# Tokens for the later experts turned by VectorE after a trip through DRAM, in place of TensorE transposes

## Chip, cores and metric

The kernel runs on one core of a Trainium2 chip. The metric is the time of one execution on the device in microseconds, the median over the runs shown.

## What is computed

Chunked attention is followed by a layer of eight experts, of which each token uses one. All is float32.

```python
# attention, chunk by chunk of 32 queries (4 batches, 8 heads, 768 positions, 64 wide)
k_full = concatenate([mem_k, k[l_start:r_end]]); v_full likewise
a = softmax(scale * q_c @ k_full.T)
out[chunk] = a @ v_full
# experts: x is the attention's output as 3072 tokens x 512
logits = x @ w_gate + modality_bias[modality_id]
e_idx = argmax(logits, 1)
gate_w = softmax(logits)[e_idx]
for e in range(8):
    h = maximum(x[e_idx == e] @ w1[e], 0)          # 512 -> 1024
    out[e_idx == e] = gate_w * (h @ w2[e])         # 1024 -> 512
```

## The kernel before

The attention runs first and leaves the tokens, with their gates, as rows of 516 floats in a DRAM scratch `xd`. Then the expert stage works in *slots*. A slot takes 256 tokens of one expert. A plan that the kernel computes on the chip, the table of *rows*, says for each row which expert and which 256 tokens it stands for, and whether its weights differ from those already loaded. Rows have fixed numbers: 0 to `HEAD` = 3, then up to eight rows of half-full tails (none here), `ROW_R1` = 12, `ROW_X` = 13, up to seven extra rows behind it (14 to 17 are used here), and 33 and 34. While a slot computes one row, it prepares the next one. So the slot that the code calls `slot(13)` prepares row 13; the last call, `slot(None)`, prepares nothing. Two slots also carry a *rest* of up to 32 more tokens; `spread` is a small constant matrix that lays these out over 128 partitions.

In a slot, `mm1(f)` for f = 0 to 7 multiplies the tokens with one eighth of `w1`: 12 matmuls, as each float32 operand is split into a rounded part and a remainder (`wh` and `wl` for weights, `xth` and `xtl` for tokens, `hh` and `hl` for what comes out) and three of the four products are taken. `mm2(f)` multiplies with `w2`, six matmuls for each f. `conv(i)` makes `wh` and `wl` of one of 16 tiles of weights `raw`: ScalarE copies, VectorE subtracts.

The tokens of the next row come by two indirect DMAs (`gather`, GpSimd's queue) into `xg`, with one token on each partition. The contraction needs them the other way round, the 512 channels on partitions. So `trans(half)` has TensorE transpose four 128x128 blocks into PSUM, from where ScalarE makes `xth` and VectorE `xtl`. This is done in `prepare(f)`, behind `mm2(2)` and `mm2(3)`.

Each engine runs its instructions in the order in which the code writes them. At a slot's head stands `begin(row)`: SP issues the loads of the next row's `w1` (`load_w(row, 0)`), ScalarE writes the finished tokens times gate to `outs` (`finish`), GpSimd scatters them to the output (`store`), copies indices and gates of the row now due (`keep`), and gathers the next row. SP's loads of `w2` (`load_w(row, 1)`) come behind `mm1`. A load waits until the conversion of what is in its buffer is through.

Of the kernel before, what the change touches and what calls it, by code (L numbers as in the profile page):

```python
# [9 lines left out]
F32 = mybir.dt.float32  # L10
F32R = mybir.dt.float32r
BF16 = mybir.dt.bfloat16
I32 = mybir.dt.int32
U32 = mybir.dt.uint32
AF = mybir.ActivationFunctionType
# [5 lines left out]
P = 128  # L21
# [25 lines left out]
NR = 32  # L47
# [5 lines left out]
def tile_chunk_attention_top1_moe(  # L53
# [31 lines left out]

    xd = dram.tile([N, XW], F32, name="xd")
    qf = q.rearrange("b h s d -> (b h s) d")
    kf = k.rearrange("b h s d -> (b h s) d")
# [100 lines left out]
    regs0 = const.tile([1, 2], I32, name="regs0")  # L189
    tab_i = const.tile([P, 193], I32, name="tab_i")  # L190
    ohg = const.tile([P, E], F32, name="ohg")

# [6 lines left out]
    def more_constants():  # L199
# [53 lines left out]
        for at in (63.5, 95.5):  # L253
            nc.vector.tensor_scalar(edge, pcol, at, None, op0=ALU.is_gt)
            nc.vector.tensor_add(quarter, quarter, edge)
            yield "v"
        nc.vector.tensor_copy(mod_f, mod_i[:, :, 0])
        yield "v"
    def bias_rows():
# [431 lines left out]
    raw, wh, wl = [None] * 16, [None] * 16, [None] * 16  # L691
    w1h, w1l = [xa.tile([P, 8, 512], F32R, name=f"w1{i}") for i in range(2)]
    for f in range(8):
        raw[f] = xa.tile([P, 512], F32, name=f"raw{f}")
        wh[f], wl[f] = w1h[:, f], w1l[:, f]
    xp = hp = xg = xth = xtl = ix = gx = hh = hl = None
    ix_now = const.tile([P, 2], I32, name="ix_now")
    gate_now = const.tile([P, 2], F32, name="gate_now")
    ev = {}

    def load_w(row, half):
        if half == 0:
            if row == 0:
                ev[0] = nc.values_load(regs0[0:1, 0:1], engines=[mybir.EngineType.SP], min_val=0, max_val=E - 1,
                                       skip_runtime_bounds_check_because="the place of one of 8 experts")
            else:
                r = (regs1 if row < 2 else regs)[row:row + 1]
                ev[row] = nc.values_load(r[:, 0:1], engines=[mybir.EngineType.SP], min_val=0, max_val=E - 1,
                                         skip_runtime_bounds_check_because="the place of one of 8 experts, or 0")
                ev[row, "c"] = nc.values_load(r[:, 1:2], engines=[mybir.EngineType.SP], min_val=0, max_val=1,  # L710
                                              skip_runtime_bounds_check_because="a comparison gives 0 or 1")
        e = ev[row]
        kw = {} if row == 0 else {"cond": ev[row, "c"]}
        for f in range(8):
            if half == 0:
                nc.sync.dma_start(
                    raw[f].rearrange("p (c f) -> p c f", f=P),
                    w1[ds(e, 1), :, f * P:(f + 1) * P].rearrange("o (c p) f -> p (o c) f", p=P), **kw)
            else:
                nc.sync.dma_start(raw[8 + f], w2[ds(e, 1), f * P:(f + 1) * P, :].rearrange("o p d -> p (o d)"), **kw)  # L720
# [5 lines left out]

    def keep():
        nc.gpsimd.tensor_copy(ix_now, ix)  # L728
        for t in range(2):
            nc.gpsimd.tensor_copy(gate_now[:, t:t + 1], xg[t][:, DM:DM + 1])  # L730
# [13 lines left out]
    def gather_rest(i):  # L744
# [7 lines left out]
        nc.gpsimd.tensor_copy(own_r[i], ixr[i])  # L752

    def trans(half):
        t = bank().rearrange("p (c n) -> p c n", c=2)
        for cc in range(2):
            for tt in range(2):
                c = 2 * half + cc
                nc.tensor.transpose(t[:, cc, tt * P:(tt + 1) * P], xg[tt][:, c * P:(c + 1) * P], ident)  # L759
        sl = slice(2 * half, 2 * half + 2)  # L760
        nc.scalar.copy(xth[:, sl, 0:256], t)  # L761
        nc.vector.tensor_sub(xtl[:, sl, 0:256], t, xth[:, sl, 0:256].bitcast(F32))

# [6 lines left out]

    def mm1(f, rest=False):
        w = 256 + (NR if rest else 0)
        pw = bank()[:, 0:w]
        ph = pw[:, 0:256]

        for n in range(12):
            wt, x, c = ((wh, xth), (wl, xth), (wh, xtl))[n // 4] + (n % 4,)
            nc.tensor.matmul(pw, wt[f][:, c * P:(c + 1) * P], x[:, c, 0:w], start=(n == 0), stop=(n == 11))  # L778
        nc.scalar.activation(hh[:, f], ph, AF.Relu)  # L779
        if rest:  # L780
            nc.scalar.activation(hq[:, f], pw[:, 256:], AF.Relu)
        nc.vector.scalar_tensor_tensor(hl[:, f], ph, 0.0, hh[:, f].bitcast(F32), op0=ALU.max, op1=ALU.subtract)  # L782
# [24 lines left out]

    def finish(t):
        nc.scalar.activation(outs[t], pos[t], AF.Copy, scale=gate_now[:, t:t + 1])  # L809

    def store():
        put = [
            nc.gpsimd.indirect_dma_start(  # L813
                out=out, out_offset=bass.IndirectOffsetOnAxis(ap=ix_now[:, t:t + 1], axis=0), in_=outs[t], in_offset=None,
                bounds_check=N - 1, oob_is_err=False)
            for t in range(2)
        ]
        tc.declare_no_dep(put[1].ins, put[0].ins, reason="the rows of different tokens")
# [141 lines left out]
    for f in range(8, 16):  # L960
# [4 lines left out]
    ixr = [hp.tile([NR, 1], I32, name=f"ixr{i}") for i in range(2)]  # L965
    gxr = hp.tile([NR, 1], I32, name="gxr")
    outs = [hp.tile([P, DM], F32, name=f"o{t}") for t in range(2)]
    hq = hp.tile([P, 8, NR], F32, name="hq")
    own_r = [hp.tile([NR, 1], F32, name=f"own_r{i}") for i in range(2)]
    ix_q = [hp.tile([P, 1], I32, name=f"ix_q{i}") for i in range(2)]  # L970
    gate_q = [hp.tile([P, 1], F32, name=f"gate_q{i}") for i in range(2)]
    spread = hp.tile([NR, P], F32, name="spread")
    nc.gpsimd.tensor_copy(
        spread.rearrange("p (a s) -> p a s", a=4), ident[0:NR, 0:NR].unsqueeze(1).to_broadcast([NR, 4, NR]))
    out_q = out.rearrange("n (a d) -> (n a) d", d=P)
# [17 lines left out]

    def begin(row, opening=False):
        if row is not None:
            load_w(row, 0)
        if not opening:
            for t in range(2):
                finish(t)
            store()  # L1000
        keep()
        if row is not None:
            gather(row)

    def prepare(f):
        for i in ((0, 1), (2, 3), (4,), (5,), (6, 7))[f] if f < 5 else ():
            conv(i)
        if f in (2, 3):
            trans(f - 2)

    def slot(row, rest=None, rest_next=None, opening=False):
        begin(row, opening)
        if rest_next is not None:
            gather_rest(rest_next)
        if not opening:
            for f in range(8):
                mm1(f, rest is not None)
                conv(8 + f)
        if rest is None and row is not None:
            load_w(row, 1)  # L1020
        for f in range(6):
# [5 lines left out]
            if opening:  # L1027
                conv(f)
                next(steps, None)
            elif row is not None:  # L1030
                prepare(f)
            if f == 3 and rest_next is not None:
# [4 lines left out]
        if row is None:  # L1037
            finish(0)
        if opening:
# [8 lines left out]
        if row is None:  # L1048
            finish(1)
            store()  # L1050

# [70 lines left out]
```

## Time and profile before

| | |
|---|---|
| median of three runs | 453.18 us (451.9 to 453.71) |
| the profiled execution, its own time | 453.23 us |
| its span in the profile | 451.4 us |
| TensorE busy | 422.2 us, 94% of the span |
| VectorE busy | 312.6 us, 69% |
| ScalarE busy | 260.4 us, 58% |
| GpSimd busy | 199.3 us, 44% |

The span is what the profiler saw of one execution; the 1.8 us to the execution's own time lie around it. Engines are PE (TensorE matmuls), PEld (its weight loads), DVE (VectorE), ACT (ScalarE), POOL (GpSimd) and SP (a queue of DMA issues). Busy shares are averages over two stages with different limits, the attention in about the first third and the experts behind it; the rows below are therefore taken from single slots.

### The profile page before, as it was taken

Reading aid. Unit: us, or ns where it says so; the run is one execution under the profiler, and the core shown is the slowest. Engines: PE = TensorE matmul, PEld = TensorE weight load, DVE = VectorE, ACT = ScalarE, POOL = GpSimd, SP = SyncE. Lnnn points to the kernel's source line nnn. Section 1 sums busy time; section 2 is a strip of 40 time slices with the busy share of each in tenths; the row PEclk is TensorE's granted clock in tenths of the full one; section 3 lists DMA queues with packets and bytes.
Section 4 is the critical chain, followed back from the end, with each engine's and each line's share of the span. In section 5 each row is a group of like instructions: output and inputs, shape, how many; then the busy total and the mean of one; then the engine's idle time right before and its main releaser. Section 6 shows DMA issues by size and latency. Waiting matters only on the chain. (4 is left out here: it accounts for less than half of the span.)

```text
span 451.4 us, 11915 instructions
## 1 busy us (share of the span) xinstructions
PE 422.2 (94%) x4109; PEld 362.7 (80%) x4109; DVE 312.6 (69%) x756; ACT 260.4 (58%) x522; POOL 199.3 (44%) x376
## 2 busy tenths in 40 slices
PE   5979998998977898999999999999999999999993
PEld 2858786786756687989798998989898989898982
DVE  8699799799897699848456455857566675848430
ACT  5566776775646663747366455656565655657521
POOL 8977779789777833214042231313040404040201
PEclk9799999999999999999999999999999999999998
DMA  7798999999877502277187834202662201120101
GB/s 198 142 231 201 227 235 210 225 229 197 188 196 187 183 2 81 61 219 235 36 242 228 237 95 166 70 1 95 187 212 69 91 5 58 40 73 23 48 0 47
DMA packets 69570, 61.74 MB, mean 137 GB/s; under 512 B 30603, under 2 KB 59491, under 8 KB 69492
## 3 DMA queue, kind: packets, MB, share of 16 engines
q1 hardware_dynamic: 62480, 41.52, 37.8%
q0 software_dynamic: 5888, 19.11, 13.9%
q8 instruction: 36, 0.59, 0.6%
q14 instruction: 42, 0.34, 0.2%
q10 hardware_dynamic: 1124, 0.18, 0.2%
HBM read 76.02 MB, written 12.76 MB: 197 GB/s over the span
## 5 line engine op out<-in xcount | busy, mean ns | idle before, releaser
L778 PEld LDWEIGHTS tr<-xt,w 128*128 128x128 f32 x1152 | 141.0, 188 | 4.9 <-issue 2.7
L778 PE MATMUL tr<-xt,w 128*128 128x256 f32 (+1 forms) x1152 | 143.0, 284 | 1.9 <-PEq L1083 0.8
L788 PE MATMUL av<-wh,h 128*128 128x512 f32 x384 | 127.8, 399 | 0.0
L813 POOL DMA_INDIRECT out_dram<-o,ix_now x24 | 24.2, 1008 | 163.9 <-ACT o L809 161.9
L782 DVE SCALAR_TENSOR_TENSOR h<-tr,h 128x256 fp32r<-128x256 f32 x96 | 40.6, 423 | 71.6 <-ACT h L779 52.7
L788 PEld LDWEIGHTS av<-wh,h 128*128 128x128 f32 x384 | 72.3, 188 | 15.5 <-issue 0.4
L788 PE MATMUL av<-wl,h 128*128 128x512 f32 x192 | 75.6, 394 | 0.0
L306 POOL COPY vw<-vw 24x384 f32<-24x384 f32 (+1 forms) x128 | 61.0, 514 | 18.1 <-DMA vw<-in_v_dram 16.7
L725 DVE TENSOR_TENSOR wl<-raw,wh 128x512 fp32r<-128x512 f32 x91 | 63.0, 692 | 8.2 <-ACT wh L723 0.9
L779 ACT ACTIVATE h<-tr 128x256 fp32r<-128x256 f32 x96 | 36.8, 384 | 51.7 <-PE tr L778 30.5
L725 DVE TENSOR_TENSOR w<-raw,w 128x512 fp32r<-128x512 f32 x93 | 60.4, 695 | 5.0 <-ACT w L723 2.5
L723 ACT CAST wh<-raw 128x512 fp32r<-128x512 f32 x96 | 58.9, 615 | 2.0 <-DMA raw<-in_moe_w_dram 2.0
L723 ACT CAST w<-raw 128x512 fp32r<-128x512 f32 x96 | 53.6, 622 | 0.0
L809 ACT ACTIVATE o<-av,gate_now 128x512 f32<-128x512 f32 x24 | 16.2, 689 | 46.6 <-PE av L788 37.2
L788 PEld LDWEIGHTS av<-wl,h 128*128 128x128 f32 x192 | 36.2, 189 | 6.5
L348 ACT COPY kbd<-tr 64x672 f32<-64x672 f32 x47 | 36.6, 779 | 6.8 <-PE tr L342 5.8
L356 PE MATMUL sc<-kbd,qT 128*32 128x128 f32 x768 | 29.5, 290 | 2.9 <-POOL kbd L330 2.9
L740 POOL DMA_INDIRECT xg<-xd,gx x24 | 26.8, 1116 | 10.6 <-POOL gx L738 6.9
L376 ACT ACTIVATE PT<-tr 128x384 f32<-128x384 f32 x32 | 15.7, 492 | 25.8 <-PE tr L374 25.3
L386 PE MATMUL av<-vw,PT 128*32 128x130 f32 x768 | 28.3, 279 | 1.9 <-ACT PT L376 1.9
L761 ACT CAST xt<-tr 128x512 fp32r<-128x512 f32 x24 | 13.9, 587 | 24.3 <-PE tr L759 13.9
L356 PEld LDWEIGHTS sc<-kbd,qT 128*32 128x32 f32 x768 | 20.5, 115 | 8.4 <-issue 4.1
(245 smaller groups left out, 531.1 us busy)
## 6 DMA issues: line engine op xcount, KB each, us to landing
raw<-in_moe_w_dram SPq DMA_DIRECT2D x192, 256.0 KB
k<-in_k_dram SPq DMA_DIRECT2D x16, 384.0 KB
q<-in_q_dram SPq DMA_DIRECT2D x16, 384.0 KB
xd<-xb POOLq DMA_DIRECT2D x16, 384.0 KB, 5.6
vw<-in_v_dram SPq DMA_DIRECT2D x32, 184.0 KB
vw<-spread_v SPq DMA_DIRECT2D x30, 48.8 KB
vw<-in_v_dram SPq DMA_DIRECT2D x32, 6.0 KB
vw<-in_v_dram SPq DMA_DIRECT2D x32, 2.0 KB
```

The lines of the kernel that those rows point to most:

```text
L306: nc.gpsimd.tensor_copy(vw[r0:r0 + 24, h, c + 1:c + 1 + w, 0:D], vw[r0 + 32:r0 + 56, h, c:c + w, 0:D])
L348: copy(dst.rearrange("p c (i j) -> p c i j", j=2)[:, :, :, j], win)
L356: nc.tensor.matmul(sc[32 * j:32 * j + 32, t * P:(t + 1) * P], qT[:, 32 * c:32 * c + 32], kbd[:, c].rearrange("p h m -> p (h m)"), start=Tr ...
L386: nc.tensor.matmul(avb[32 * j:32 * j + 32, t * W:(t + 1) * W], PT[:, t * P + 32 * j:t * P + 32 * j + 32], vw[:, :, c], start=True, stop=True,)
L723: nc.scalar.copy(wh[i], raw[i])
L725: (eng or nc.vector).tensor_sub(wl[i][:, s], raw[i][:, s], wh[i][:, s].bitcast(F32))
L740: nc.gpsimd.indirect_dma_start(out=xg[t], out_offset=None, in_=xd[0:rows], in_offset=bass.IndirectOffsetOnAxis(ap=gx[:, t:t + 1], axis=0))
L778: nc.tensor.matmul(pw, wt[f][:, c * P:(c + 1) * P], x[:, c, 0:w], start=(n == 0), stop=(n == 11))
L779: nc.scalar.activation(hh[:, f], ph, AF.Relu)
L782: nc.vector.scalar_tensor_tensor(hl[:, f], ph, 0.0, hh[:, f].bitcast(F32), op0=ALU.max, op1=ALU.subtract)
L788: nc.tensor.matmul(pos[t], x, w[8 + f], start=(f == 0 and n == 0), stop=(f == 7 and n == 2))
L813: nc.gpsimd.indirect_dma_start(out=out, out_offset=bass.IndirectOffsetOnAxis(ap=ix_now[:, t:t + 1], axis=0), in_=outs[t], in_offset=None, ...
```

## The change

Rows from `ROW_X` on are no longer transposed by TensorE. `bounce()` writes the gathered tokens from `xg` to a DRAM scratch `xs` and reads them back as `xq`: partition 32a + s holds token s of each group of 32 tokens, and of that token the quarter a of the channels. `turn(half)` has VectorE transpose all 32x32 blocks of 128x512 into `xv`, and `turned(half)` makes `xth` and `xtl` from that. In `xv` the channels lie in another order on partitions and tiles than before, so `w1` is loaded to match for these rows: one DMA now fills 32 partitions of four tiles, in runs of 512 floats where it was 128. `mm1` picks its weights accordingly, as many matmuls as before. The load of `w1` for row 13 is made whatever is in the buffer, since the layout changes there.

In `begin`, `keep` and the gather now stand ahead of `finish` and `store`; `keep` has a second pair of buffers (`ix_out`, `gate_out`) for the tokens still to be stored. `spread` is made by VectorE among the attention's constants, and no more by GpSimd at the stages' border.

```diff
     def load_w(row, half):
...
-        kw = {} if row == 0 else {"cond": ev[row, "c"]}
+        kw = {} if row == 0 or row == ROW_X and half == 0 else {"cond": ev[row, "c"]}
         for f in range(8):
-            if half == 0:
+            if half == 0 and row < ROW_X:
                 nc.sync.dma_start(
                     raw[f].rearrange("p (c f) -> p c f", f=P),
                     w1[ds(e, 1), :, f * P:(f + 1) * P].rearrange("o (c p) f -> p (o c) f", p=P), **kw)
+            elif half == 0:
+                src = w1[ds(e, 1), :, (f // 4) * DM:(f // 4 + 1) * DM]
+                c = f % 4
+                nc.sync.dma_start(
+                    raw1[32 * c:32 * c + 32, f - c:f - c + 4],
+                    src[:, c * P:(c + 1) * P].rearrange("o (c s) f -> s (o c) f", s=32), **kw)
...
-    def keep():
+    def keep(opening):
+        if not opening:
+            nc.gpsimd.tensor_copy(ix_out, ix_now)
+            nc.gpsimd.tensor_copy(gate_out, gate_now)
         nc.gpsimd.tensor_copy(ix_now, ix)
...
+    def split(x, sl, cols):
+        nc.scalar.copy(xth[:, sl, cols], x)
+        nc.vector.tensor_sub(xtl[:, sl, cols], x, xth[:, sl, cols].bitcast(F32))
+
+    def bounce():
+        for t in range(2):
+            nc.sync.dma_start(xs[t * P:(t + 1) * P], xg[t][:, 0:DM])
+        for a in range(4):
+            nc.sync.dma_start(
+                xq[32 * a:32 * a + 32], xs[:, a * P:(a + 1) * P].rearrange("(j s) d -> s j d", s=32))
+
+    def turn(half):
+        nc.vector.transpose(
+            xv.rearrange("p c (t j s) -> p t j c s", t=2, j=4)[:, half],
+            xq[:, 4 * half:4 * half + 4].rearrange("p j (c s) -> p j c s", c=4))
+
+    def turned(half):
+        sl = slice(2 * half, 2 * half + 2)
+        split(xv[:, sl], sl, slice(0, 256))
...
-    def mm1(f, rest=False):
+    def mm1(f, rest=False, whole=True):
...
-            nc.tensor.matmul(pw, wt[f][:, c * P:(c + 1) * P], x[:, c, 0:w], start=(n == 0), stop=(n == 11))
+            i, j = (f, c) if whole else (f - f % 4 + c, f % 4)
+            nc.tensor.matmul(pw, wt[i][:, j * P:(j + 1) * P], x[:, c, 0:w], start=(n == 0), stop=(n == 11))
...
-    def begin(row, opening=False):
+    def begin(row, opening=False, rest_next=None):
         if row is not None:
             load_w(row, 0)
+        keep(opening)
+        if row is not None:
+            gather(row)
+            if rest_next is not None:
+                gather_rest(rest_next)
+            if row >= ROW_X:
+                bounce()
         if not opening:
             for t in range(2):
-                finish(t)
-            store()
-        keep()
-        if row is not None:
-            gather(row)
+                finish(t, gate_out)
+            store(ix_out)

-    def prepare(f):
+    def prepare(f, whole=True):
+        if f in (2, 3) and not whole:
+            turn(f - 2)
         for i in ((0, 1), (2, 3), (4,), (5,), (6, 7))[f] if f < 5 else ():
             conv(i)
-        if f in (2, 3):
+        if f in (2, 3) and whole:
             trans(f - 2)
+        if f in (3, 4) and not whole:
+            turned(f - 3)
```

On VectorE, the second half of the slot that prepares row 34, before (`w` is a tile of weights' remainders, `xt` is `xtl`, the last row belongs to the next slot's `mm1`):

```order
L725 TENSOR_TENSOR w_197<-raw_202,w_196 128x512
L762 TENSOR_TENSOR xt_2729<-tr,xt_2728 128x2x256
L725 TENSOR_TENSOR w_197<-raw_203,w_196 128x512
L762 TENSOR_TENSOR xt_2729<-tr,xt_2728 128x2x256
L725 TENSOR_TENSOR w_197<-raw_204,w_196 128x512
L725 TENSOR_TENSOR w_197<-raw_205,w_196 128x512
L782 SCALAR_TENSOR_TENSOR h_2731<-tr,h_2730 128x256
```

and after:

```order
L737 TENSOR_TENSOR w_199<-raw,w_198 128x512 x4
L781 STREAM_TRANSPOSE xv<-xq 128x4x4x32
L737 TENSOR_TENSOR w_199<-raw,w_198 128x512
L781 STREAM_TRANSPOSE xv<-xq 128x4x4x32
L737 TENSOR_TENSOR w_199<-raw,w_198 128x512
L771 TENSOR_TENSOR xt_2727<-xv,xt_2726 128x2x256
L737 TENSOR_TENSOR w_199<-raw,w_198 128x512 x2
L771 TENSOR_TENSOR xt_2727<-xv,xt_2726 128x2x256
L816 SCALAR_TENSOR_TENSOR h_2729<-tr,h_2728 128x256
```

The two transposes stand ahead of the fifth and the sixth weight tile, and the second half of `xtl` has moved behind the last weight tile.

On GpSimd, from the scatter of one slot to that of the next (`regs` is the plan's table), before:

```order
L813 DMA out_dram<-o_2980,ix_now 3072x512
L813 DMA out_dram<-o_2981,ix_now 3072x512
L728 COPY ix_now<-ix 128x2
L730 COPY gate_now<-xg_2726 128x1
L730 COPY gate_now<-xg_2727 128x1
L735 TENSOR_LOAD regs
L737 ISA
L737 COPY ix<-tab_i 128x2
L738 TENSOR_SCALAR gx<-ix 128x2
L740 DMA xg_2726<-xd,gx 128x516
L740 DMA xg_2727<-xd,gx 128x516
```

and after (`ix_201` and `gate_203` are `ix_now` and `gate_now`, `ix_202` and `gate_204` are `ix_out` and `gate_out`):

```order
L847 DMA out_dram<-o_2981,ix_202 3072x512
L741 COPY ix_202<-ix_201 128x2
L742 COPY gate_204<-gate_203 128x2
L743 COPY ix_201<-ix 128x2
L745 COPY gate_203<-xg_2724 128x1
L745 COPY gate_203<-xg_2725 128x1
L750 TENSOR_LOAD regs
L752 ISA
L752 COPY ix<-tab_i 128x2
L753 TENSOR_SCALAR gx<-ix 128x2
L755 DMA xg_2724<-xd,gx 128x516
L755 DMA xg_2725<-xd,gx 128x516
```

The order in the program is nearly the same; what has moved is which slot's scatter comes behind a gather. Before, the scatter that opens a slot stood ahead of that slot's gather; now it stands behind it.

On SP, in the same slot of the changed kernel, the last load of `w1`, `bounce`, and the first loads of `w2` (`raw_2949` and on; an ISA row decides whether the load behind it is made):

```order
L728 ISA
L728 DMA raw<-in_moe_w_dram 32x4x512
L775 DMA xs<-xg_2724 128x512
L775 DMA xs<-xg_2725 128x512
L777 DMA xq<-xs 32x8x128 x4
L732 ISA
L732 DMA raw_2949<-in_moe_w_dram 128x512
```

The six DMAs of `bounce` are new in this queue, between `w1` and `w2`.

## Rows read from the trace of the kernel before

**Rows 1.** The page, part 2: busy tenths of engines and clock in 40 slices.

```profile
PE   5979998998977898999999999999999999999993
DVE  8699799799897699848456455857566675848430
PEclk9799999999999999999999999999999999999998
```

**Rows 2.** Chain of waits, one slot: start us, length us, engine, tile, line, count.

```profile
397.67 11.40 PE tr L778 x96
409.06 4.20 PE av L788 x18
413.27 0.44 PE tr L759 x4
413.70 1.39 PE av L788 x6
415.09 0.44 PE tr L759 x4
415.53 5.51 PE av L788 x24
```

**Rows 3.** Timeline of TensorE: start us, length us, engine, line, operation, out<-in, count.

```profile
303.25 11.56 PE L778 MATMUL tr<-xt,w 128*128 128x256 f32 x96
...
397.50 11.56 PE L778 MATMUL tr<-xt,w 128*128 128x256 f32 x96
...
420.87 11.56 PE L778 MATMUL tr<-xt,w 128*128 128x256 f32 x96
...
443.23 0.39 PE L788 MATMUL av<-wh,h 128*128 128x512 f32 x1
```

**Rows 4.** Tile xg: count and ns (lowest/median/highest) of one; the gathers' landing.

```profile
L759 PE MATMUL tr<-ident,xg x96: 270/272/328, 143.3 to 415.3; 128*128 128x128 f32 x96
...
DMA to landing us min/median/max: 3.4/3.8/5.4
```

**Rows 5.** Timeline of VectorE, second half of a slot; in brackets idle time before.

```profile
316.43 3.09 DVE L725 TENSOR_TENSOR w<-raw,w 128x512 fp32r<-128x512 f32 x5
320.14 0.69 DVE L762 TENSOR_TENSOR xt<-tr,xt 128x512 fp32r<-128x512 f32 x1 [0.62 <-ACT xt L761]
...
321.97 0.69 DVE L762 TENSOR_TENSOR xt<-tr,xt 128x512 fp32r<-128x512 f32 x1 [0.54 <-ACT xt L761]
322.58 1.28 DVE L725 TENSOR_TENSOR w<-raw,w 128x512 fp32r<-128x512 f32 x2
```

**Rows 6.** VectorE by line and shape: count, busy us, mean ns of one.

```profile
L348 DVE COPY kbd<-tr 64x672 f32<-64x672 f32 x17 | 14.7, 862 | 1.8 <-ACT kbd L348 1.4
L311 DVE COPY qr<-q 128x768 f32<-128x768 f32 x16 | 9.9, 616 | 0.0
```

**Rows 7.** Timeline of SP's queue, weight loads of one row.

```profile
317.99 6.49 SPq L716 DMA_DIRECT2D raw<-in_moe_w_dram  x8
```

**Rows 8.** DMA issues: queue, count, median us from issue to landing.

```profile
out_dram<-o,ix_now POOLq DMA_INDIRECT x24, 2.8
```

**Rows 9.** Timeline of GpSimd: the copy of spread, and the gather of one slot.

```profile
148.62 0.30 POOL L973 COPY spread<-ident 32x128 f32<-32x128 f32 x1
...
307.45 0.55 POOL L728 COPY ix_now<-ix 128x2 int32<-128x2 int32 x1 [1.90 <-DMA out_dram<-o,ix_now]
...
309.18 1.40 POOL L740 DMA_INDIRECT xg<-xd,gx  x1 [0.51 <-POOL gx L738]
310.89 0.96 POOL L740 DMA_INDIRECT xg<-xd,gx  x1 [0.30 <-PE tr L778]
```

**Rows 10.** Stretches: busy us of PE, PEld, DVE, ACT, POOL, clock, DMA share, GB/s.

```profile
324.00:326.00 2.00, 2.00 (x11) 1.63 (x10) 0.00 (x0) 0.42 (x1) 0.00 (x0) 1.00 1.01 279
326.00:328.00 2.00, 2.00 (x16) 1.88 (x15) 0.00 (x0) 0.95 (x2) 1.10 (x2) 1.00 0.48 132
...
397.70:421.00 23.30, 23.30 (x154) 21.16 (x153) 15.14 (x26) 13.85 (x28) 5.21 (x10) 1.00 0.14 47
```

More of the change, by code (lines that the diff above doesn't have):

```diff
@@ L86, in tile_chunk_attention_top1_moe @@
     xd = dram.tile([N, XW], F32, name="xd")
+    xs = dram.tile([2 * P, DM], F32, name="xs")
     qf = q.rearrange("b h s d -> (b h s) d")
@@ L190, in tile_chunk_attention_top1_moe @@
     tab_i = const.tile([P, 193], I32, name="tab_i")
+    spread = const.tile([NR, P], F32, name="spread")
     ohg = const.tile([P, E], F32, name="ohg")
@@ L257, in more_constants @@
         nc.vector.tensor_copy(mod_f, mod_i[:, :, 0])
+        yield "v"
+        nc.vector.tensor_copy(
+            spread.rearrange("p (a s) -> p a s", a=4), ident[0:NR, 0:NR].unsqueeze(1).to_broadcast([NR, 4, NR]))
         yield "v"
@@ L692, in tile_chunk_attention_top1_moe @@
     w1h, w1l = [xa.tile([P, 8, 512], F32R, name=f"w1{i}") for i in range(2)]
+    raw1 = xa.tile([P, 8, 512], F32, name="raw")
     for f in range(8):
-        raw[f] = xa.tile([P, 512], F32, name=f"raw{f}")
+        raw[f] = raw1[:, f]
         wh[f], wl[f] = w1h[:, f], w1l[:, f]
     xp = hp = xg = xth = xtl = ix = gx = hh = hl = None
-    ix_now = const.tile([P, 2], I32, name="ix_now")
-    gate_now = const.tile([P, 2], F32, name="gate_now")
+    ix_now, ix_out = [const.tile([P, 2], I32, name=f"ix_{i}") for i in range(2)]
+    gate_now, gate_out = [const.tile([P, 2], F32, name=f"gate_{i}") for i in range(2)]
     ev = {}
@@ L759, in trans @@
                 nc.tensor.transpose(t[:, cc, tt * P:(tt + 1) * P], xg[tt][:, c * P:(c + 1) * P], ident)
-        sl = slice(2 * half, 2 * half + 2)
-        nc.scalar.copy(xth[:, sl, 0:256], t)
-        nc.vector.tensor_sub(xtl[:, sl, 0:256], t, xth[:, sl, 0:256].bitcast(F32))
+        split(t, slice(2 * half, 2 * half + 2), slice(0, 256))
     def trans_rest(i):
@@ L806, in spread_rest, with finish, store @@
         nc.vector.tensor_copy(gate_q[i], t[:, 1:2])
-    def finish(t):
-        nc.scalar.activation(outs[t], pos[t], AF.Copy, scale=gate_now[:, t:t + 1])
-    def store():
+    def finish(t, gate):
+        nc.scalar.activation(outs[t], pos[t], AF.Copy, scale=gate[:, t:t + 1])
+    def store(to):
         put = [
             nc.gpsimd.indirect_dma_start(
-                out=out, out_offset=bass.IndirectOffsetOnAxis(ap=ix_now[:, t:t + 1], axis=0), in_=outs[t], in_offset=None,
+                out=out, out_offset=bass.IndirectOffsetOnAxis(ap=to[:, t:t + 1], axis=0), in_=outs[t], in_offset=None,
                 bounds_check=N - 1, oob_is_err=False)
@@ L966, in tile_chunk_attention_top1_moe @@
     gxr = hp.tile([NR, 1], I32, name="gxr")
+    xq = hp.tile([P, 8, P], F32, name="xq")
+    xv = hp.tile([P, 4, 256], F32, name="xv")
     outs = [hp.tile([P, DM], F32, name=f"o{t}") for t in range(2)]
@@ L971, in tile_chunk_attention_top1_moe @@
     gate_q = [hp.tile([P, 1], F32, name=f"gate_q{i}") for i in range(2)]
-    spread = hp.tile([NR, P], F32, name="spread")
-    nc.gpsimd.tensor_copy(
-        spread.rearrange("p (a s) -> p a s", a=4), ident[0:NR, 0:NR].unsqueeze(1).to_broadcast([NR, 4, NR]))
     out_q = out.rearrange("n (a d) -> (n a) d", d=P)
@@ L992, in tile_chunk_attention_top1_moe @@
     pump(99, True)
-    def begin(row, opening=False):
+    def begin(row, opening=False, rest_next=None):
         if row is not None:
             load_w(row, 0)
+        keep(opening)
[5 more added lines that the diff above has]
+                bounce()
         if not opening:
             for t in range(2):
-                finish(t)
-            store()
-        keep()
-        if row is not None:
-            gather(row)
-    def prepare(f):
+                finish(t, gate_out)
[3 more added lines that the diff above has]
+            turn(f - 2)
         for i in ((0, 1), (2, 3), (4,), (5,), (6, 7))[f] if f < 5 else ():
             conv(i)
-        if f in (2, 3):
+        if f in (2, 3) and whole:
             trans(f - 2)
+        if f in (3, 4) and not whole:
+            turned(f - 3)
     def slot(row, rest=None, rest_next=None, opening=False):
-        begin(row, opening)
-        if rest_next is not None:
-            gather_rest(rest_next)
+        begin(row, opening, rest_next)
         if not opening:
             for f in range(8):
-                mm1(f, rest is not None)
+                mm1(f, rest is not None, row is not None and row <= ROW_X)
                 conv(8 + f)
@@ L1030, in slot @@
             elif row is not None:
-                prepare(f)
+                prepare(f, row < ROW_X)
             if f == 3 and rest_next is not None:
@@ L1037, in slot @@
         if row is None:
-            finish(0)
+            finish(0, gate_now)
         if opening:
@@ L1048, in slot @@
         if row is None:
-            finish(1)
-            store()
+            finish(1, gate_now)
+            store(ix_now)
     def short_slot(row):
```

## The prediction

> **What bounds the kernel now.** I read the page's busy times and slices first [rows 1]. [...] So in the expert stage, which is where the change lies, TensorE sets the pace, and only two things can move the time: fewer matmuls, or something that makes TensorE wait.
>
> The chain of waits confirms it for a whole slot [rows 2]: nothing but TensorE's own work, one piece behind the other, 11.40 + 4.20 + 0.44 + 1.39 + 0.44 + 5.51 = 23.38 us. The two pieces of 0.44 us are `trans(0)` and `trans(1)`, four transposes each. The reader is to see that they stand in the chain, not beside it.
>
> **What the removed transposes are worth.** The plain price is 2 x 0.44 = 0.88 us a slot. But the same rows say that this is too much. Ahead of the transposes 18 matmuls of `mm2` take 4.20 us (0.233 each); behind them 24 take 5.51 (0.230 each). The timeline of TensorE has a slot without transposes, the last one, which prepares nothing [rows 3]: from its first `mm1` at 420.87 to its last `mm2` at 443.23 plus 0.23 for that matmul is 22.59 us, where the slot before it runs from 397.50 to 420.87, 23.37 us. The difference is 0.78 us, not 0.88: without transposes the matmuls keep the slower pace to the end. I take 0.78, and 0.88 as the upper bound.
>
> How often: 96 transposes were run [rows 4], 8 for each of 12 rows of tokens. The changed path serves all rows from `ROW_X` on; rows 0, 1, 2, 3 and `ROW_R1` keep the old one. That leaves 12 - 5 = 7 slots, 7 x 0.78 = **5.5 us** (7 x 0.88 = 6.2 at most).
>
> **VectorE.** It gets two transposes of 128x512 a slot, each of a duration T that no row shows, and loses two waits. In the second half of the slot that starts at 303.25 [rows 3] it makes [rows 5] five subtractions at 0.62 us apiece from 316.43, waits 0.62 for ScalarE's copy of the first transposed half, subtracts, makes one more of the weights, waits 0.54, subtracts, and ends at 322.58 + 1.28 = 323.86. The new order has the same ten subtractions and 2T: it starts at 316.43 as before, since what stands ahead is `mm1`'s output, and ends at 316.43 + 10 x 0.62 + 2T = 322.63 + 2T. Its last result, the second half of `xtl`, is read first by the ninth matmul of the next slot's `mm1(0)`. That slot now starts at 303.25 + 23.37 - 0.78 = 325.84, and eight matmuls at 11.40 / 96 = 0.119 us later it is 326.79. So TensorE waits only if T is over (326.79 - 322.63) / 2 = 2.08 us. Bounds for T from rows [rows 6]: a plain copy of 128x768 takes 616 ns, 0.41 us for 512 columns; the copy with scattered addresses takes 862 ns for 672 columns, 0.66 for 512; a transposition that filled and emptied its array by turns at that slower rate would take 1.3. I take 0.69, the row of the same shape that VectorE runs here. All of it lies under 2.08, so the term is 0, with 2.8 us of VectorE's time to spare at T = 0.69. The work that hides it is `mm2`; without that cover it would cost 2T a slot, 9.7 us over seven.
>
> [...]
>
> **The round trip by DRAM.** `xq` must be there when `turn(0)` comes up, behind four subtractions: 316.43 + 4 x 0.62 = 318.91, which is 15.7 us after the slot's first matmul. With VectorE's 2.8 us to spare, TensorE starts to wait if `xq` lands later than 18.5 us into the slot. Where does it come from? In SP's queue `bounce` stands behind the eight `w1` loads of the same row. Those end their issue at 317.99 + 6.49 = 324.48 [rows 7], 2.1 us before the next slot's start at 303.25 + 23.37 = 326.62, as the last of them waits for VectorE's last subtractions. The write of `xs` I price by the output stores, 2.8 us to landing for 256 KB [rows 8], the reads into `xq` by the gathers, 3.8 us for 256 KB [rows 4]: both halves at once, or one after the other, give 6.6 to 13.2 us. So `xq` lands 4.5 to 11.1 us into the slot: 4.6 us early at the worst. Term 0.
>
> That needs the gathered rows by then, and here the order on GpSimd matters. Before, the stores stand ahead of the gather, and behind the stores `ix_now` waits 1.9 us for them to land, so a row's gather is issued 6 to 9 us into its own slot (309.18, and 310.89 + 0.96 for the second half) [rows 9]. After, `keep` and the gather stand ahead of the stores, so that behind the stores of slot n comes at once the gather of slot n + 1: the same 6 to 9 us, but a whole slot earlier. Each gather only has to wait until `xs` was written from the same buffer. What waits behind it on GpSimd is the next slot's store, which is not due until that slot starts.
>
> **Slots that load new weights.** Only two of the seven load `w1` from DRAM: row 13, and the one whose load starts at 317.99, where DMA moves 279 GB/s and then 132 while stores join; a slot without loads has 47 GB/s [rows 10], which over 23.3 us is 1.1 MB, its gather and its stores. There the second 1 MB of `w1` (four tiles, released together now, as each DMA fills 32 partitions of four tiles) lies in front of `xs`. It takes 3.8 us at 279 GB/s and 7.9 at 132, so `xq` lands at 8.3 to 19.0 us; the 0.5 MB of stores, at 132 GB/s, can add 4. Against 18.5 that is a stall of 0 to 4.5 us in each of two slots. The middle, about 14, is in time, so 0.
>
> [...]
>
> **The rest.** The eight loads of `w1` are as many as before, with runs of 2 KB in place of 512 bytes; that lies on SP and behind matmuls. Two more small copies of `keep` on GpSimd (0.6 us or less each, as `ix_now`'s [rows 9]) are hidden in its idle time. `spread` moves from GpSimd, 0.30 us [rows 9], to VectorE in the attention stage, where VectorE is up to 9 tenths busy: 0 to 0.3 us, I take 0. The end of the kernel is untouched.
>
> **Sum.** The profiled execution took 453.23 us for a span of 451.4; the median of the runs shown is 453.18, 0.05 less. 453.23 - 5.46 = **447.8 us**.
>
> **Rivals.** (a) *Partly late*: the two loading slots lose 1 to 4 us together; for it the 132 GB/s and the 32 partitions, against it the 17.8 us between issue and need. 447.8 + 1 to 4 = 449 to 452. (b) *No gain*: the transposes fill a gap of TensorE that some other limit leaves, so that the time stays, 452 to 454. Against it stands the last slot, which is shorter by 0.78 us. (c) *Slower, VectorE*: T of four passes of the 0.69 us row, 2.76 us, would put VectorE's end 1.4 us a slot after the need; less the 0.78 gained, 7 x 0.62 = 4.3 us slower than before, 457.5. It decides from T = 2.08 + 0.39 = 2.47 on. (d) *Slower, round trip*: if the gather does not get ahead (`keep` or the shared `xg` holds it in its own slot), it lands at about 8.6 + 3.8 = 12.4 us, and `xq` at 19.0 to 25.6; at 20.5 that is 2 us late in seven slots, 447.8 + 14 = 462. It decides from 19.3 us on. Against it the order of GpSimd's rows.
>
> **How the numbers follow.** My forecast gets 0.70, and alone runs from 446.4 (0.88 a slot, and a run as far below the median as the fastest of before) to 449. (a) gets 0.12, (b) 0.06, (c) 0.05, (d) 0.07. From 446.4 to 450.9 lie the forecast and half of (a) or more, about 8 in 10. Half a per cent, 2.3 us, is about what a measurement of this kernel can tell from no change: faster is below 450.9, forecast and most of (a), 0.81; same 0.08; slower 0.11.
>
> **What would show it.** Right: a chain of waits in slots 13 on with one piece of `mm2` of 48 in about 11.2 us, slots of 22.6 us, VectorE's transposes well below 2 us with no wait ahead of them, gathers issued a slot early, `xq` landed by 12 us. Wrong: TensorE waiting at a slot's start for `xt`, VectorE waiting for a DMA ahead of a transpose, or SP's `w2` loads pushed so far back by `bounce` that the next slot's conversions wait.

## The result, and the profile after

| | before | after |
|---|---|---|
| median, six runs of each in one comparison | 452.02 us (451.09 to 453.71) | 446.19 us (444.95 to 447.79) |
| ratio | | 0.9868, 95% interval 0.9845 to 0.9891 |
| profiled execution | 453.23 us, span 451.4 | 445.03 us, span 443.2 |

The kernel became 5.8 us faster, 1.3%. The forecast was faster, 447.8 us; the result lies 0.21 us below the lower end of the range.

The page of the changed kernel, part 2, answers to [rows 1]:

```profile
PE   6979999998988898999999999999999999999993
...
DVE  8799799798787699857646376686858594959530
...
PEclk9899999999979999999999999999999999999998
```

TensorE still sets the pace of the expert stage, at a granted clock of 1.00 from 250 to 435 us, and VectorE, with 14 transposes more, still has room. So the time must have gone out of TensorE's own stream. Its timeline in the changed kernel (columns as in [rows 3]; `mm1` is now line 812, `mm2` 822):

```profile
251.03 12.95 PE L812 MATMUL tr<-xt,w 128*128 128x288 f32 x96
...
277.07 11.52 PE L812 MATMUL tr<-xt,w 128*128 128x256 f32 x96
...
299.58 11.52 PE L812 MATMUL tr<-xt,w 128*128 128x256 f32 x96
...
413.00 11.52 PE L812 MATMUL tr<-xt,w 128*128 128x256 f32 x96
...
435.27 0.40 PE L822 MATMUL av<-wh,h 128*128 128x512 f32 x1
```

From 277.07 to 299.58 a slot takes 22.51 us. For the whole I take one *stretch* in all kernels below: from the first `mm1` of the slot that computes row 12, the first that prepares a row in the new way, to the end of the last `mm2`, 0.23 us after its last matmul's start. After: 435.27 + 0.23 - 251.03 = 184.47 us. Before, the same slot's `mm1` started at 253.18, in the row of its timeline that follows, and the last `mm2` ended at 443.23 + 0.23 = 443.46 [rows 3]: 190.28 us.

```profile
253.18 12.96 PE L778 MATMUL tr<-xt,w 128*128 128x288 f32 x96
```

The difference, **5.81 us**, is the whole of the difference of the medians, 5.83. Up to the last slot's start it is (420.87 - 253.18) - (413.00 - 251.03) = 5.72 us, on average 0.82 for each of the seven slots; the last slot gave 0.09.

The two profiled executions differ by more, 8.20 us, since the stretch also began 2.15 us earlier. No run shows that to be the change's doing: kernels with the same code ahead of it began it at 250.49, 252.83 and 254.35 us (the repeat, and the experiments with four-fold and with idle transposes).

VectorE, second half of the slot that starts at 277.07, answers to [rows 5]:

```profile
290.22 2.49 DVE L737 TENSOR_TENSOR w<-raw,w 128x512 fp32r<-128x512 f32 x4
292.63 0.70 DVE L781 STREAM_TRANSPOSE xv<-xq 128x512 f32<-128x512 f32 x1
293.26 0.65 DVE L737 TENSOR_TENSOR w<-raw,w 128x512 fp32r<-128x512 f32 x1
293.83 0.70 DVE L781 STREAM_TRANSPOSE xv<-xq 128x512 f32<-128x512 f32 x1
294.45 0.65 DVE L737 TENSOR_TENSOR w<-raw,w 128x512 fp32r<-128x512 f32 x1
295.27 0.69 DVE L771 TENSOR_TENSOR xt<-xv,xt 128x512 fp32r<-128x512 f32 x1 [0.17 <-ACT xt L770]
295.88 1.29 DVE L737 TENSOR_TENSOR w<-raw,w 128x512 fp32r<-128x512 f32 x2
297.09 0.69 DVE L771 TENSOR_TENSOR xt<-xv,xt 128x512 fp32r<-128x512 f32 x1
```

T is 0.70 us, and no bracket stands at a transpose: `xq` is there when its turn comes. VectorE ends at 297.78; the ninth matmul of the next slot, which reads that, starts at 299.58 + 8 x 0.119 = 300.53, 2.75 us later (the prediction: 2.8).

GpSimd in that slot, answering to [rows 9]:

```profile
281.14 0.69 POOL L741 COPY ix<-ix 128x2 int32<-128x2 int32 x1 [1.86 <-DMA out_dram<-o,ix]
...
283.57 1.04 POOL L755 DMA_INDIRECT xg<-xd,gx  x1 [0.28 <-POOL gx L753]
284.91 0.97 POOL L755 DMA_INDIRECT xg<-xd,gx  x1 [0.30 <-DMA raw<-in_moe_w_dram]
299.49 1.02 POOL L847 DMA_INDIRECT out_dram<-o,ix  x1 [13.61 <-ACT o L843]
```

The wait of 1.86 us for the stores is still there, and the gather behind it is issued 6.5 us into the slot as before. But it is now the gather of a slot later: the next store stands behind it and waits 13.6 us for its data, so the gather is a whole slot ahead.

SP's queue, answering to [rows 7], with the slots that start at 299.58 and 322.14:

```profile
292.84 5.64 SPq L728 DMA_DIRECT2D raw<-in_moe_w_dram  x8
298.58 0.83 SPq L775 DMA_DIRECT2D xs<-xg  x2
301.36 1.98 SPq L777 DMA_DIRECT2D xq<-xs  x4
...
315.35 6.60 SPq L728 DMA_DIRECT2D raw<-in_moe_w_dram  x8
322.06 0.84 SPq L775 DMA_DIRECT2D xs<-xg  x2
328.46 1.93 SPq L777 DMA_DIRECT2D xq<-xs  x4
```

The write to `xs` is issued 1.0 us ahead of the first slot and 0.1 ahead of the second; the last read into `xq` 3.8 us into the first, and 8.25 us into the second, whose weights come from DRAM. There the windows show (columns as in [rows 10]):

```profile
316.00:318.00 2.00, 2.00 (x11) 1.59 (x10) 1.83 (x4) 0.87 (x2) 0.00 (x0) 1.00 0.76 207
318.00:320.00 2.00, 2.00 (x10) 1.64 (x9) 2.00 (x4) 1.31 (x3) 0.00 (x0) 1.00 1.06 212
320.00:322.00 2.00, 2.00 (x10) 1.59 (x9) 0.28 (x1) 0.69 (x1) 0.00 (x0) 1.00 1.04 210
```

The loads into 32 partitions move 207 to 212 GB/s, with the DMA engines fully taken in the last two windows (a share of 1.06 and 1.04), where loads into 128 moved 279 [rows 10]. These loads also have longer runs than before, and no run tells the two apart. The rate costs nothing, as the turn comes 15.6 us into the slot.

The other slot that loads, where row 13 is prepared from 251.03 us on, is tighter:

```profile
256.22 1.82 SPq L775 DMA_DIRECT2D xs<-xg  x2
262.94 1.80 SPq L777 DMA_DIRECT2D xq<-xs  x4
```

The write to `xs` is issued 5.2 us into this slot and the last read 13.7 us; VectorE's transpose comes 19.6 us into it, at 270.66, and waits for nothing.

### The profile page after: what moved, and what is told of

It is laid out like the page before. It is cut to its first block, busy times and chain, and to the rows that moved or that the text cites. A ratio compares the mean times of both kernels' runs of the same rounds, so it can differ in the third digit from the quotient of the medians.

```text
span 443.2 us, 11870 instructions
## 1 busy us (share of the span) xinstructions
PE 417.8 (94%) x4053; PEld 356.9 (81%) x4053; DVE 320.3 (72%) x771; ACT 260.1 (59%) x522; POOL 205.2 (46%) x397
## 5 line engine op out<-in xcount | busy, mean ns | idle before, releaser
L822 PE MATMUL av<-wh,h 128*128 128x512 f32 x384 | 124.9, 397 | 0.0
L847 POOL DMA_INDIRECT out_dram<-o,ix x24 | 24.7, 1030 | 93.6 <-ACT o L843 91.1
L843 ACT ACTIVATE o<-av,gate 128x512 f32<-128x512 f32 x24 | 16.2, 689 | 38.9 <-PE av L822 30.7
L391 PEld LDWEIGHTS av<-vw,PT 128*32 128x32 f32 x768 | 19.7, 109 | 6.5 <-ACT PT L381 4.6
```

Source lines behind the costliest of these rows:

```text
L391: nc.tensor.matmul(avb[32 * j:32 * j + 32, t * W:(t + 1) * W], PT[:, t * P + 32 * j:t * P + 32 * j + 32], vw[:, :, c], start=True, stop=True,)
L822: nc.tensor.matmul(pos[t], x, w[8 + f], start=(f == 0 and n == 0), stop=(f == 7 and n == 2))
L847: nc.gpsimd.indirect_dma_start(out=out, out_offset=bass.IndirectOffsetOnAxis(ap=to[:, t:t + 1], axis=0), in_=outs[t], in_offset=None, boun ...
```

## The experiments

The runs fall into three sets, each beside runs of the kernel before on the same chip. That took 453.61 us in the first (new order alone, `spread` back, old order, idle transposes), 452.19 in the second (the repeat, `spread` in its old place, gaps, four-fold transposes) and 452.25 in the third (the rest). Ratios are against these.

**The order alone.** The new order in `begin` and the early `spread` stay; all rows are transposed by TensorE, with `w1` in its old layout and without the tiles `xs`, `xq` and `xv`.

```diff
-            if half == 0 and row < ROW_X:
+            if half == 0 and row < 99:
...
-            if row >= ROW_X:
+            if row >= 99:
...
-                prepare(f, row < ROW_X)
+                prepare(f, row < 99)
```

> The order of the changed kernel (keep and gather ahead of the stores, spread made early), but TensorE transposes in all slots and w1 in the old layout. Theory A, the gain is the removed TensorE work in seven slots and nothing else: no gain, ratio 0.998 to 1.002, about 452 us. Rival B, the earlier gathers or the earlier spread give a part of the 5.8 us: 449 to 451 us, ratio 0.993 to 0.997.

454.16 us, ratio 1.000 (0.9975 to 1.0026); the stretch took 190.51 us. The reorder by itself is worth nothing: the theory that the gain comes from an earlier gather or the earlier `spread` falls.

**TensorE's transposes put back, with nobody waiting for them.** The changed kernel, plus eight transposes a slot of a constant that nothing reads.

```diff
+        if f in (2, 3) and not whole:
+            t = bank()
+            for i in range(4):
+                nc.tensor.transpose(t[:, i * P:(i + 1) * P], ident, ident)
```

> The changed kernel with eight TensorE transposes of a constant put back where trans stood, their results unused; nothing waits for them. Theory A: seven slots are longer by 0.78 to 0.88 us again, 451.7 to 452.4 us, ratio 0.999 to 1.001. Rival B, part of the gain is not TensorE's transposes but the wait for data or the new order: 448 to 451 us.

453.26 us, ratio 0.9991 (0.9967 to 1.0015); stretch 190.48 us. The whole gain is gone, by TensorE's time alone: all of the new path is still there, and TensorE waits no longer than in the changed kernel. Against this run and the one above, the changed kernel's stretch is 6.0 us shorter, 0.86 for each of seven slots (one profile of each).

**The old order with the new path.** Finishing, stores and the copy of indices ahead of the gather again.

```diff
-        keep(opening)
+        if not opening:
+            for t in range(2):
+                finish(t, gate_now)
+            store(ix_now)
+        keep(True)
```

> The changed kernel with begin in the old order: stores, then keep, gather and the trip through DRAM. Theory A, as the prediction had it for rival d: a gather lands 12.4 us into its own slot and xq 6.6 to 13.2 us later, so VectorE waits for a DMA ahead of its first transpose and TensorE waits 0.5 to 7 us in each of seven slots, 450 to 495 us, middle about 473. Rival C, the trip is so short that the order does not matter: 446 to 447 us, no wait on VectorE.

462.53 us, ratio 1.0152 (1.0096 to 1.0208), from four runs, of which one took 456.99 and three 462.43 to 462.96. In the slot that starts at 304.49, `xs` is issued only at 316.67, and VectorE waits:

```profile
324.97 0.71 DVE L781 STREAM_TRANSPOSE xv<-xq 128x512 f32<-128x512 f32 x1 [3.56 <-DMA xq<-xs]
```

Of VectorE's waits (27.7 us in seven) 7.8 us come through to TensorE. The stretch grew more, to 452.70 + 0.23 - 255.95 = 196.98 us, 12.5 over the changed kernel's. TensorE's timeline of this kernel behind the longest wait, and the windows there:

```profile
354.94 0.50 PE L812 MATMUL tr<-xt,w 128*128 128x256 f32 x2 [3.13 <-ACT xt L770]
356.50 12.89 PE L812 MATMUL tr<-xt,w 128*128 128x256 f32 x94 [1.06 <-ACT xt L770]
```

```profile
356.00:358.00 2.00, 1.50 (x7) 1.50 (x8) 1.42 (x3) 1.61 (x3) 0.69 (x1) 0.62 0.93 340
358.00:360.00 2.00, 2.00 (x11) 2.00 (x11) 0.42 (x1) 0.89 (x2) 1.34 (x2) 0.53 0.53 212
360.00:362.00 2.00, 2.00 (x19) 2.00 (x18) 1.22 (x3) 0.89 (x2) 0.48 (x4) 1.00 0.25 99
```

After the wait the granted clock stands at 0.53 to 0.62 before it is back at 1.00; `mm1` takes 12.89 us for 94 matmuls where 96 take 11.52. Of the four slots at whose head TensorE waits, two show this, behind 4.2 and 2.1 us of waits; behind 1.1 and 0.5 us the clock stays at 1.00, and 94 matmuls take 11.29 and 11.45 us. Summed in windows over the stretch (TensorE's busy time, times what the clock lacks to 1), the low clock costs an estimated 3.4 us. With the 7.8 us of waits that leaves 1.3 of the 12.5 us.

**Each VectorE transpose four times.**

```diff
+        for _ in range(4):
-        nc.vector.transpose(
+            nc.vector.transpose(
```

> Each of VectorE's two transposes a slot run four times. The changed kernel's profile has VectorE's last result of a slot at 297.78 us and its first use at about 300.53, 2.75 us to spare; six more transposes at 0.61 to 0.70 add 3.7 to 4.2. Theory A: TensorE waits 0.9 to 1.5 us in six or seven slots, 6 to 10 us more than the changed kernel, ratio 1.000 to 1.009. Rival: ScalarE and VectorE make it up in mm1's half or the room is larger, ratio 0.986 to 0.990.

463.04 us, ratio 1.0226 (1.0185 to 1.0266), above what was expected. Four transposes take 2.95 us, so a slot has 4.5 us more of VectorE's work than the 2 x 0.70 of the changed kernel: 1.75 beyond the room of 2.75. TensorE's waits are of that size:

```profile
PE tr L813 <- ACT xt L770: 7.8, 8, 1.1
PE tr L813 <- ACT o L844: 2.7, 1, 2.7
```

(In such a row stand the sum, the number and the longest of the waits.) In six slots a wait of 1.05 or 1.06 us stands at the third matmul of `mm1`, which reads ScalarE's copy of the second transposed half, and not at the ninth, which reads VectorE's last result:

```profile
304.62 0.61 ACT L770 CAST xt<-xv 128x512 fp32r<-128x512 f32 x1
```

```profile
305.29 11.28 PE L813 MATMUL tr<-xt,w 128*128 128x256 f32 x94 [1.06 <-ACT xt L770]
```

In the changed kernel that copy ends at 296.81, and the third matmul starts at 299.58 + 2 x 0.119 = 299.82, 3.0 us later; of the 4.5 us, 1.5 lie beyond. The 2.7 us put down to ScalarE's `o` are one slot's, and no run shows how much of them VectorE made.

All waits sum to 10.5 us; the stretch, from 252.83 to 453.59, grew by 200.76 - 184.47 = 16.3. Part of the rest lies again in low clock, behind two of the seven slots' waits, as in these windows:

```profile
354.00:356.00 2.00, 1.70 (x9) 1.70 (x10) 1.22 (x3) 1.41 (x3) 0.89 (x1) 0.65 0.00 0
356.00:358.00 2.00, 2.00 (x11) 2.00 (x11) 0.82 (x2) 0.89 (x2) 1.14 (x2) 0.50 0.65 256
```

The clock fell behind 2.0 and 2.7 us of waits and stayed at 1.00 behind the 1.1 to 1.6 us of the other five slots, where 94 matmuls took 11.28 to 11.45 us. By the same sum it costs an estimated 3.4 us. Between 2 and 3 us are left; the last matmul ahead of each stop lasts 0.40 to 0.51 us, where inside a row one follows the other after 0.23 or 0.12, which would make an estimated 0.44 us a slot, 3 us in seven.

The room is real, and behind it rival (c) begins, dearer than I had it.

**The changed kernel again.** No edit; another chip.

> The changed kernel unaltered, for a second profile and as the measure of this set. Theory A: ratio 0.985 to 0.989; seven slots of 22.4 to 22.7 us where rows 2 have 23.4; the start of the expert stage's first slots differs from the first profile by up to 2 us, since the runs of one kernel differ by that much before the experts begin. Rival: the lead of 2.3 us at that point in the first profile belongs to the change and comes again.

444.57 us, ratio 0.9837 (0.9803 to 0.9872); the stretch from 250.49 on took 184.50 us, against 184.47. The stretch repeats to 0.03 us where whole times of the same code differ by a microsecond or more. This comparison's interval is a gain of 5.8 to 8.9 us; whether some of that lies ahead of the stretch is not shown.

**`spread` back to GpSimd at the border of the stages.** Its tile is in the pool `hp` again, behind the new `xq` and `xv`.

```diff
-    spread = const.tile([NR, P], F32, name="spread")
...
+    spread = hp.tile([NR, P], F32, name="spread")
+    nc.gpsimd.tensor_copy(
+        spread.rearrange("p (a s) -> p a s", a=4), ident[0:NR, 0:NR].unsqueeze(1).to_broadcast([NR, 4, NR]))
```

> The changed kernel with spread made by GpSimd at the border of the stages again. Theory A: as the changed kernel, 446.2 us, ratio 0.987. Rival B, the 2.3 us by which the changed kernel's profile was ahead when the expert stage's matmuls began come from this: 448 to 448.5 us, ratio 0.991 to 0.992, and the first long run of mm1 begins some 2 us later than in the changed kernel's profile.

455.53 us, ratio 1.0043 (1.0014 to 1.0072). No theory had that number: a copy of 0.28 us takes the whole gain and more. GpSimd, then VectorE, then TensorE at that place:

```profile
154.34 0.28 POOL L1005 COPY spread<-ident 32x128 f32<-32x128 f32 x1 [4.69 <-PE tr L556]
154.60 8.34 POOL L733 TENSOR_TENSOR wl<-raw,wh 128x128 fp32r<-128x128 f32 x20
```

```profile
154.89 8.12 DVE L560 TENSOR_TENSOR l<-l,btok 128x48 f32<-128x48 f32 x1
```

```profile
164.69 0.32 PE L588 MATMUL tr<-oh,ones_b 128*128 128x48 bf16 x6 [6.04 <-DVE oh L577]
```

The stretch takes 184.52 us here, so all of the loss lies ahead of it. The copy now waits 4.69 us for a TensorE transpose of the gate's logits, though it reads only a constant; before, it waited for nothing [rows 9]. GpSimd's 20 subtractions behind it start at 154.60 (in the changed kernel 148.06). VectorE's small add, part of what picks each token's expert, is then held until they end, 8.12 us; in the changed kernel it takes 0.39. TensorE waits 6.04 us for what follows.

**`spread` at the border, in its old place in `hp`**, with `xq` and `xv` behind it, so that it might get its old memory back.

```diff
+    spread = hp.tile([NR, P], F32, name="spread")
...
+    xq = hp.tile([P, 8, P], F32, name="xq")
+    xv = hp.tile([P, 4, 256], F32, name="xv")
```

> spread made by GpSimd at the border of the stages as before, but with xq and xv laid behind it in memory, so that it lies where it lay before the change. Theory D, that run e2_spread_back lost its 8 us because spread came to lie on memory that TensorE's transposes of the router's numbers read late: the copy waits less than 0.5 us, no long VectorE instruction, ratio 0.985 to 0.990. Rival E, that GpSimd's copy costs by itself wherever spread lies: ratio 1.000 to 1.006.

453.77 us, ratio 1.0038 (1.0013 to 1.0062). It did not help: the copy still waits, and the add takes 5.98 us. This order of tiles does not bring back the old state, so the run does not decide whether memory is the reason.

```profile
152.53 0.28 POOL L1003 COPY spread<-ident 32x128 f32<-32x128 f32 x1 [6.29 <-PE tr L546]
```

**Gaps in GpSimd's run.** `spread` back in `hp` as above, and a small memset behind each of the 20 subtractions.

```diff
+            if eng and i >= 8:
+                nc.gpsimd.memset(gap, 0.0)
```

> Run e2_spread_back with a small memset on GpSimd behind each of the 20 subtractions of w2 that GpSimd makes. Theory F, that these subtractions, when they run without a pause, keep VectorE's addition of two SBUF operands (8.12 us in place of 0.2 to 0.4) from starting until the last is through: with gaps it runs in under 1 us, TensorE's wait of 6.0 us there falls under 1 us, ratio 0.987 to 0.992. Rival G, that VectorE is held for another reason, a semaphore or memory: the instruction is as long as GpSimd's run again, 8 us or more, ratio 1.004 or more.

455.52 us, ratio 1.0055 (1.0028 to 1.0083). The add takes 8.77 us, from 154.39 to 163.16, and GpSimd's last instruction ends at 163.13. Twenty changes of instruction on GpSimd did not let it in.

```profile
153.91 0.28 POOL L1008 COPY spread<-ident 32x128 f32<-32x128 f32 x1 [5.06 <-PE tr L557]
154.18 0.45 POOL L734 TENSOR_TENSOR wl<-raw,wh 128x128 fp32r<-128x128 f32 x1
```

**`spread` at the border, by GpSimd, but in the pool `const`.** Only the memory differs from the run that lost the gain.

```diff
-        nc.vector.tensor_copy(
-            spread.rearrange("p (a s) -> p a s", a=4), ident[0:NR, 0:NR].unsqueeze(1).to_broadcast([NR, 4, NR]))
-        yield "v"
...
+    nc.gpsimd.tensor_copy(
+        spread.rearrange("p (a s) -> p a s", a=4), ident[0:NR, 0:NR].unsqueeze(1).to_broadcast([NR, 4, NR]))
```

> The changed kernel with spread in the memory that the change gives it, free from the start, but made by GpSimd at the border of the stages, where it stood before. Theory H, what cost 8 us in runs e2_spread_back and e12_spread_first is the wait of GpSimd's queue (4.7 and 6.3 us) for memory that others still read, which puts its run of 20 subtractions on top of VectorE's work for the router: no wait, no long VectorE instruction, ratio 0.982 to 0.988. Rival I, the copy at this place costs whatever its memory: ratio 1.000 or more.

445.91 us, ratio 0.9868 (0.9833 to 0.9904), the changed kernel's own; stretch 184.46 us. GpSimd and VectorE:

```profile
147.74 0.81 POOL L1005 COPY spread<-ident 32x128 f32<-32x128 f32 x1
149.07 8.88 POOL L734 TENSOR_TENSOR wl<-raw,wh 128x128 fp32r<-128x128 f32 x20 [0.53 <-ACT wh L732]
```

```profile
153.83 0.40 DVE L561 TENSOR_TENSOR l<-l,btok 128x48 f32<-128x48 f32 x1
```

Same engine, same place, no wait: it is where the tile lies that made the copy late. That its memory was still held by TensorE's work is read from what released the copy's wait.

**More rows in the new way.** Three kernels begin earlier: row 3 too (eight slots); rows 3 and 12 (nine); rows 2 and 3 (nine). The rests must follow the order of channels, by 16 small matmuls in place of four transposes. The diff is that of rows 3 and 12; the other two keep row 12, and the second rest, as they were.

```diff
-            nc.tensor.transpose(t[:, c], xgr[i][:, c * P:(c + 1) * P], ident[0:NR, 0:NR])
+            for a in range(4):
+                nc.tensor.matmul(
+                    t[32 * a:32 * a + 32, c], xgr[i][:, a * P + 32 * c:a * P + 32 * c + 32], ident[0:NR, 0:NR],
+                    start=True, stop=True)
...
-            wsl = [w[:, 4 * half:4 * half + 4, c * P:(c + 1) * P] for w in (w1h, w1l)]
+            wsl = [w[:, 4 * half + c, :] for w in (w1h, w1l)]
...
-            if row >= ROW_X:
+            if row >= 3:
```

> The new path for row 3 and from row 13 on, in eight slots; row 12 in the old one, with the change of layout at rows 3, 12 and 13. In the changed kernel's trace row 3's gather is issued by 196.1 and its w1 by 195.7 us, so xq should land near 207, ahead of the need at 213.5. Theory A: in time, 0.8 us less than the changed kernel less about 0.2 for 12 more small matmuls, ratio 0.9815 to 0.986. Rival: late by the loads of both weights in that slot, ratio 0.986 to 0.995, VectorE waits for a DMA there.

444.75 us, ratio 0.9838 (0.9814 to 0.9862). The slot that prepares row 3 takes 24.03 us, where it takes 24.74 to 25.16 in the kernels above that leave it alone.

> The new path from row 3 on, so in nine slots, with the rests' tokens brought into the same order of channels by 16 small matmuls. If only TensorE's work counted: 1.5 us less than the changed kernel, ratio 0.981 to 0.984. [...]

444.44 us, ratio 0.9821 (0.979 to 0.9853), the fastest of all. The slot that prepares row 12 falls from 27.94 to 27.21 us. VectorE waits there, within its 2.75 us, and TensorE does not:

```profile
244.44 0.71 DVE L781 STREAM_TRANSPOSE xv<-xq 128x512 f32<-128x512 f32 x1 [2.17 <-DMA xq<-xs]
```

Both whole times overlap the changed kernel's interval; the slots are what tells them apart from it.

> As the run before with row 2 as well, nine slots. Row 2's gather is issued at 180.0 to 182.3 us in the changed kernel's trace, xq lands then about 192 where the need is 190.5, with 2.75 us of VectorE's time behind it. Theory A: just in time, 1.4 us less than the changed kernel, ratio 0.980 to 0.985. Rival: late by 1 to 4 us, ratio 0.986 to 0.996.

451.70 us, ratio 0.9985 (0.9959 to 1.0012). Row 2 comes too late: VectorE waits 8.41 us for `xq`, and TensorE 4.8 us where the next slot begins. From the end of the `mm2` ahead of it (197.94) that slot takes 31.8 us, 7.7 over the 24.0 of the same slot with row 2 left as it was. VectorE's timeline and TensorE's waits:

```profile
199.25 0.71 DVE L784 STREAM_TRANSPOSE xv<-xq 128x512 f32<-128x512 f32 x1 [8.41 <-DMA xq<-xs]
```

```profile
PE tr L821 <- ACT xt L773: 4.8, 2, 4.0
```

## Why the prediction was right, and where it was off

**What bounds the kernel, and what the transposes are worth: right in kind.** TensorE stands at 9 tenths without a break from 181 us to the last slice but one [rows 1]. Its own work was the bound, and its removal is the gain: idle transposes put back take all of it, the order without the new path gives none. Rival (b) falls by both.

**The size, 0.78 a slot: too small.** Seven slots gave 0.82 each on average (0.76 to 0.97), and the last slot, which I took as the picture of a slot without transposes, itself became 0.09 shorter, from 22.59 to 22.50. So it was no clean measure: its matmuls are the same in all kernels, and where nothing made it wait it took 22.39 to 22.60 us. The chain's 0.88, which I kept as a bound, was off by 0.06 where 0.78 was off by 0.04, and the 0.86 by which idle transposes and new order alone differ from the changed kernel lies next to it. Together this is 5.81 - 5.46 = 0.35 us.

**The base, 453.23: the step that failed by most.** The sum began from the profiled execution, 453.23, and the three runs shown agreed with it. Six runs have the median 452.02, 1.21 lower. 1.21 and the 0.35 above make 1.56 of the 1.58 us by which 447.77 was too high. Part of that is the draw of the runs: the three shown are among the six, and larger sets of the same kernel have medians of 453.61, 452.19 and 452.25, with times from 450.17 to 456.15.

**The lower end, 446.4: a slip.** It was to allow for 0.88 a slot and also for a run as far below the median as the fastest of before. Both together give 453.23 - 6.16 - 1.28 = 445.8; 446.4 is the fastest run less 5.46, so it allows for one of the two. The bound of 445.8 would have held 446.19.

**VectorE, T = 0.69: right.** 0.70 measured; the room of 2.75 us is as forecast. The 0.69 was the row of another operation, taken out of bounds of 0.41 to 1.3, the upper an estimate of mine that no run shows, so that it came so near is partly luck; any T in the bounds gives the same term. Rival (c) did not come. The four-fold transposes bear out its mechanism in the main: TensorE waits, by about the 1.5 us that lie beyond the room. But the wait showed at the third matmul, behind ScalarE's copy, which I had not counted among the consumers, and the price was too low, since I counted the wait and not what comes on top of it.

**The round trip and the order on GpSimd: right.** The gather runs a slot ahead, and the last read was issued 3.8 us into the slot. No row shows its landing; where VectorE had to wait for `xq` in other kernels, it came 2.2 to 3.5 us behind the last issue, which makes an estimated 6 to 7.3 us here, inside my 4.5 to 11.1. Rival (d), forced by the old order, cost 8.9 us against before by the medians (6.9 by the ratio), where I had 462 - 453.2 = 8.8. That the numbers are so near is luck: in the stretch, which repeats better, it cost 196.98 - 190.28 = 6.7 us against before. The parts were other than I said as well: not 2 us in each of seven slots, but 7.8 us of waits in four of them, an estimated 3.4 of low clock and 1.3 more, less the gain.

**Loading slots: right, rival (a) did not come.** `bounce` began on SP between 1.0 us ahead of a slot and, for row 13, 5.2 us into it, where I had 2.1 ahead. The last reads of the two loading slots were issued at 8.25 and 13.7 us; with 2.2 to 3.5 us to landing that is an estimated 10.5 to 17.2, inside my 8.3 to 19.0. That loads into 32 partitions are slower, which I named for rival (a), was read from no row; they then moved 207 to 212 GB/s, between my 132 and 279.

**`spread`, 0 to 0.3 us: right number, missed reason.** I priced the copy and not its place in memory. The new tiles make `hp` larger; with `spread` still in it the change would have ended at 1.0043 instead of 0.9868. No rival of mine had this.

What stays open: why VectorE's add is held to the end of GpSimd's run in three kernels, and takes 0.39 us in the middle of the same run, started earlier, in the changed kernel.

## What to carry to other kernels

When one engine's stream is the chain, work can move to an engine that does it more slowly (here 0.70 us for 0.44), if its data is fetched a slot ahead; count the spare time of each consumer, since what comes later than that costs TensorE the wait and, behind waits of 2.0 us and more in these runs, low clock on top. When a change adds tiles to a pool, look in the new trace at the first writer of every other tile in that pool: a copy that reads only constants and yet waits, as here for 4.69 to 6.29 us, may have been laid on memory still in use. Begin the sum from the median of many runs, and compare kernels over the stretch that the change touches, which repeated to 0.03 us here.

## What the runs showed of the hardware

**Waits of TensorE cost about 1.6 times their length here.** 7.8 us of waits lengthened the stretch by 12.5 (old order), 10.5 by 16.3 (four-fold transposes), and 4.8 one slot by 7.7 (rows 2 and 3 too). Low clock is an estimated 3.4 us in each of the first two. In windows of 2 us the granted clock fell to 0.50 to 0.53 behind 2.0, 2.1, 2.7 and 4.2 us of waits at a slot's head; it stayed at 1.00 behind 0.5 to 1.6 us, where the 94 matmuls behind the wait took 11.28 to 11.45 us. Behind the 4.8 us they took 13.35.

**VectorE's add of `btok` to `l` was held for 5.98, 8.12 and 8.77 us**, each time to the end of a run of 20 GpSimd subtractions of 0.42 to 0.45 us, so for the length of fourteen to twenty of them. In the kernel before, in the changed one and its repeat, and with `spread` made by GpSimd in `const`, the same add took 0.39 to 0.41 us in the middle of such a run. No run shows the reason.
